# Attention scores as three rounded products of split q and k, with the unit's steps rearranged

## The chip, the cores and the metric

The program runs on one core of a Trainium2 chip. The metric is the device time in microseconds of one execution. Kernels are compared by the median of several runs. The profile comes from one further execution, whose own time is given beside its span.

## The reference, cut to what matters

Attention over 4 batches, 8 heads, 576 positions and 64 columns a head, with a bias that a small network computes from positions; then two feed-forward layers over 2304 tokens of width 512 (2048 and 1536 inner columns). All inputs and the output are float32.

```
scores = q @ k.T / sqrt(64)                                  # B, H, S, S
x      = log1p(|i - j|) / log1p(max(i, 1))
scores = scores + (relu(x @ w1 + b1) @ w2) per head          # the bias
attn   = softmax(scores);  o = attn @ v                      # B, H, S, 64
x      = o as (2304, 512)
h = x @ w_in;  x = (h * cos(h)) @ w_out                      # first layer
xn = rms_norm(x) * rms_g
out = (silu(xn @ w_gate) * (xn @ w_val)) @ w_out             # second layer
```

## The kernel before

The order of all instructions is written out by hand; each engine executes its own in that order, and semaphores on tiles hold an instruction until what it reads has been written and what it overwrites has been read.

There are three stages. The bias stage (the loop over `T`, 36 turns) makes features of 128 partitions by 576 columns, three of four on VectorE (L413) and one on ScalarE (L415), multiplies them on TensorE (L443), scales the result on ScalarE (L449) and writes it to memory; `load_bias` reads it back by heads. The features run two turns ahead. Three steps of the first attention unit are put into this loop, at T = 28, 31 and 35 (`STEP_AT`).

The attention stage runs over 16 units. A unit `u` is a pair of heads of one batch; its 9 row tiles of 576 queries (2 heads by 4.5 tiles of 128) are worked off in five steps `p`. In steps 0 to 3, `qk` (L217) computes the scores of a query tile of both heads: the two heads lie on partitions 0 to 63 and 64 to 127, and their matmuls run side by side on two halves of the rows of the array (row tiling, `tile_position=(64 * hh, 0)`). Step 4 takes the last half tiles of both heads in one matmul of full height (L222). All of this is float32, which is two instructions a matmul in the profile. `softmax` then adds the bias and takes the row maximum on VectorE (L231), which empties the PSUM tile of the scores (two such buffers), and takes the exponential and the row sum on ScalarE (L235). `tr` transposes the tile on TensorE against `ident` (L247, L251; L257, L260 for step 4) through three PSUM buffers, and copies it to `eT` on ScalarE and VectorE (L248, L252, L258). `av` multiplies by v (L278) with the two heads on two halves of the array's columns (column tiling), in two halves of a unit of 256 and 320 queries, each over five chunks of keys. `recip` takes the reciprocals of the sums, and has GpSimd spread them (`rw`, L290); `norm` transposes `rw` (L298), and `norm_out` multiplies (L313), rounds to float32r on ScalarE (`xh`, L315) and takes the remainder on GpSimd (`xl`, L316).

In `step(u, p)` the transposes are those of the step before (`tr(u, p - 1)`, in step 0 `tr(u - 1, 4)`), and `av` runs in all five steps: chunks 3 and 4 of the last unit's first half in step 0, its second half in steps 1 and 2, the first half of this unit's in steps 3 and 4. `load_k` and `load_q` put q and k of the next unit into double buffers in step 1.

The feed-forward stage (`run_item`, 140 items) multiplies by `mm3` (L508): both factors are split into a rounded float32r part and its remainder, and three of the four products are added up in PSUM. The weights come as 64-bit numbers in 68 pieces: `w_abs` on ScalarE (L105), `w_conv` on VectorE in two calls of two instructions each (L116 and L117, L120 and L121), `w_split` on ScalarE and GpSimd (L137, L138) into a ring of 1 + 9 buffers (`WA`, `WB`). From unit 4 on, two calls of `w_conv` and one of `w_tick` stand in each attention unit.

Of the kernel before, what the change touches and what calls it, by code (L numbers as in the profile page):

```python
# [7 lines left out]
F32 = mybir.dt.float32  # L8
F32R = mybir.dt.float32r
# [14 lines left out]
SPAN = 2 * S - 4  # L24
BLKS = [(0, 512), (512, 512), (2048, 256), (1024, 512), (1536, 512)]
# [6 lines left out]
WB = 9  # L32
# [19 lines left out]
def attn_moe(tc, qd, kd, vd, smallp, lrow, ident_d, wf1, wf2, rmsg, out):  # L52
# [56 lines left out]
    def w_conv():  # L109

        i = wstate["conv"]
        r = raw_t[i]
        hi, lo = r[:, :, 1], r[:, :, 0]
        t = w32_t[i]
        if not wstate["half"]:
            nc.vector.tensor_scalar(t.bitcast(F32), t.bitcast(F32), LEAST, GREATEST, op0=ALU.max, op1=ALU.min)  # L116
            nc.vector.tensor_scalar(t, t, 3, 0x3FFFFFFF, op0=ALU.logical_shift_left, op1=ALU.bitwise_and)  # L117
            wstate["half"] = 1
            return
        nc.vector.scalar_tensor_tensor(t, hi, -0x40000000, t, op0=ALU.bitwise_and, op1=ALU.bitwise_or)  # L120
        nc.vector.scalar_tensor_tensor(t, lo, 29, t, op0=ALU.logical_shift_right, op1=ALU.bitwise_or)  # L121
        raw_t.pop(i)
        wstate["half"] = 0
        wstate["conv"] += 1

    def w_split(eng=nc.gpsimd):
        i = wstate["split"]
        j = i % (WA + WB)
        if j < WA:
            t = wa.tile([128, 2, 512], F32R, tag="w", name="wA", bufs=WA)  # L130
        else:
# [38 lines left out]
    def load_k(u):  # L170
        if u < 16:
            hp, b = divmod(u, 4)
            kt = prep.tile([128, 640], F32, tag="k", name="kt", bufs=2)
            nc.sync.dma_start(kt, kd[b, hp])
            kq[u] = [kt, None]

    def load_q(u):
        if u < 16:
            hp, b = divmod(u, 4)
            qt_ = prep.tile([128, 640], F32, tag="q", name="qt", bufs=2)  # L180
            nc.sync.dma_start(qt_, qd[b, hp])
            kq[u][1] = qt_
# [20 lines left out]
    prep, st_prep = pool("prep")  # L203

    st = {}

    def qk(u, p):


        kt, qt_ = kq[u]  # L210
        if p < 4:
            pss = [psB.tile([128, 2, 512], F32, tag="S", name="psS", bufs=2) for _ in range(2)]
            for x in range(2):
                for hh in range(2):
                    r = slice(64 * hh, 64 * hh + 64)
                    k0 = 64 - 64 * hh + 288 * x
                    nc.tensor.matmul(pss[hh][:, x, 0:288], qt_[r, 128 * p:128 * p + 128], kt[r, k0:k0 + 288],  # L217
                                     start=True, stop=True, tile_position=(64 * hh, 0))
            return pss
        ps = psB.tile([128, 2, 512], F32, tag="S", name="psS", bufs=2)  # L220
        for x in range(2):
            nc.tensor.matmul(ps[:, x, 0:288], qt_[:, 512:640], kt[:, 64 + 288 * x:352 + 288 * x], start=True, stop=True)  # L222
        return [ps]
# [14 lines left out]
    def tr(u, p):  # L238
        s_ = st[u]
        e = s_["e"].pop(p)  # L240
        if p < 4:
            eT, q0 = (s_["eT0"], 128 * p) if p < 2 else (s_["eT1"], 128 * (p - 2))
            for c, ev in ((0, nc.scalar.copy), (2, nc.vector.tensor_copy)):
                pt = psA.tile([128, 512], F32, tag="tr", name="pt", bufs=3)
                for i in range(4):
                    k0 = 128 * (c + i // 2) + (S + 64) * (i % 2)
                    nc.tensor.transpose(pt[:, 128 * i:128 * i + 128], e[:, k0:k0 + 128], ident)  # L247
                ev(eT[:, 2 * c:2 * c + 4, q0:q0 + 128], pt.rearrange("p (c q) -> p c q", c=4))  # L248

            pt = psA.tile([128, 512], F32, tag="tr", name="pt", bufs=3)  # L250
            nc.tensor.transpose(pt[:, 0:128], e[:, 512:640], ident)  # L251
            nc.vector.tensor_copy(eT[:, 8, q0:q0 + 128], pt[:, 0:128])  # L252
        else:
            eT = s_["eT1"]
            pt = psA.tile([128, 512], F32, tag="tr", name="pt", bufs=3)
            for c in range(4):
                nc.tensor.transpose(pt[:, 128 * c:128 * c + 128], e[:, 128 * c:128 * c + 128], ident)  # L257
            nc.scalar.copy(eT[:, 0:8, 256:320], pt.rearrange("p (c q) -> p c q", c=8))  # L258
            pt = psA.tile([128, 512], F32, tag="tr", name="pt", bufs=3)
            nc.tensor.transpose(pt[:, 0:128], e[:, 512:640], ident)  # L260
            nc.vector.tensor_copy(eT[0:64, 8, 256:320], pt[0:64, 0:64])
            nc.vector.tensor_copy(eT[64:128, 8, 256:320], pt[64:128, 64:128])
# [30 lines left out]
    def norm(u, half):  # L293
        s_ = st[u]
        rp = psA.tile([128, 512], F32, tag="tr", name="rp", bufs=3)
# [4 lines left out]
        nc.scalar.copy(rbc[:, 0:256], rp[:, 0:256])  # L300
        s_["rbc", half] = rbc
# [5 lines left out]
    def norm_out(u, half):  # L307
# [4 lines left out]
        xt = ap.tile([128, 320], F32, tag="xt", name="xt", bufs=2)  # L312
# [15 lines left out]
    def step(u, p):  # L328
# [29 lines left out]
        if p == 2:
            if u > 0:
                av(u - 1, 1, [3, 4])  # L360
            recip(u, 0)
        if p == 4:
            av(u, 0, [2])
        if p == 3:
            av(u, 0, [0, 1])
        if p == 1 and u > 0:
            load_k(u + 1)
            load_q(u + 1)
        if u >= 4 and p in (0, 3):
# [56 lines left out]
    load_k(0)  # L426
    load_q(0)
# [4 lines left out]
    for T in range(NTT):  # L432
# [258 lines left out]
    def run_item(n, between=None):  # L691
# [18 lines left out]
        w_tick(lambda i: i < WA + WB or lastuse[pieces[i - WA - WB]] <= n - SPL,  # L710
# [4 lines left out]
    def rest():  # L715
        norm(15, 1)
# [89 lines left out]
```

## Time and profile before

| | |
|---|---|
| median of 3 runs | 1192.57 us (1191.5 to 1192.88) |
| profiled execution, own time | 1192.12 us |
| its span | 1190.3 us |
| bias stage with the first unit | 0 to about 72 us |
| attention, units 1 to 15 | about 72 to 333 us |
| feed-forward | about 333 us to the end |
| TensorE busy | 1173.7 us (99%) |
| VectorE, ScalarE, GpSimd busy | 825.6, 542.1, 351.6 us |
| granted TensorE clock | 1.00 in every stretch |

How to read it: PE is TensorE's matmuls, PEld its weight loads, DVE VectorE, ACT ScalarE, POOL GpSimd, SP SyncE, which issues DMAs. Ends of matmuls are modelled and overlap the next one's start, so distances from start to start tell the pace. L217 is line 217 of the kernel before.

### The profile page before, as it was taken

Reading aid. Unit: us, or ns where it says so; the run is one execution under the profiler, and the core shown is the slowest. Engines: PE = TensorE matmul, PEld = TensorE weight load, DVE = VectorE, ACT = ScalarE, POOL = GpSimd, SP = SyncE. Lnnn points to the kernel's source line nnn. Section 1 sums busy time; section 2 is a strip of 40 time slices with the busy share of each in tenths; the row PEclk is TensorE's granted clock in tenths of the full one; section 3 lists DMA queues with packets and bytes.
Section 4 is the critical chain, followed back from the end, with each engine's and each line's share of the span. In section 5 each row is a group of like instructions: output and inputs, shape, how many; then the busy total and the mean of one; then the engine's idle time right before and its main releaser. Section 6 shows DMA issues by size and latency. Waiting matters only on the chain.

```text
span 1190.3 us, 17685 instructions
## 1 busy us (share of the span) xinstructions
PE 1173.7 (99%) x6628; PEld 907.4 (76%) x6628; DVE 825.6 (69%) x1588; ACT 542.1 (46%) x1060; POOL 351.6 (30%) x373
## 2 busy tenths in 40 slices
PE   7999999999999999999999999999999999999998
PEld 3466666666678888888888887888888888888887
DVE  8966677777778789879879987885565355533232
ACT  7966667767654444445435546332222222222111
POOL 0011112222232244234234445663331232123111
PEclk9999999999999999999999999999999999999999
DMA  6833425362212011201201110111112011200012
GB/s 194 267 120 108 135 66 160 103 191 65 69 37 70 19 36 36 71 19 37 70 18 43 46 36 18 50 58 36 36 36 74 16 46 43 71 1 1 36 46 78
DMA packets 30852, 79.23 MB, mean 67 GB/s; under 512 B 3888, under 2 KB 4144, under 8 KB 30768
## 3 DMA queue, kind: packets, MB, share of 16 engines
q1 hardware_dynamic: 30480, 77.52, 20.8%
q8 instruction: 52, 0.85, 0.3%
q10 hardware_dynamic: 288, 0.59, 0.1%
q14 instruction: 32, 0.26, 0.1%
HBM read 62.76 MB, written 15.34 MB: 66 GB/s over the span
## 4 chain that ended last, share of the span: by engine, by line
PE 85%; DVE 8%; ACT 3%; issue 2%; DMA 1%; POOL 0%; SPq 0%; DVEq 0%; ACTq 0%; POOLq 0%
PE y L508 25%; PE h L508 13%; PE hg L508 12%; PE hv L508 12%; PE o L278 7%; PE psS L217 6%; PE pt L247 5%; PE psS L222 1%; DVE ft L413 1%; PE psb L443 1%; ACT G L449 1%; DVE yacc L611 1%; PE pt L257 1%; PE rp L298 1%; PE pt L251 1%
## 5 line engine op out<-in xcount | busy, mean ns | idle before, releaser
L508 PE MATMUL y<-g,wB 128*128 128x512 f32 (+1 forms) x960 | 213.4, 370 | 1.7 <-DVE yacc L611 1.2
L508 PEld LDWEIGHTS y<-g,wB 128*128 128x128 f32 x960 | 167.6, 188 | 34.4 <-DVE yacc L611 2.8
L558 POOL TENSOR_TENSOR g<-t,g 128x512 fp32r<-128x512 f32 (+1 forms) x80 | 98.1, 1227 | 236.8 <-ACT g L557 236.8
L575 POOL TENSOR_TENSOR g<-t,g 128x512 fp32r<-128x512 f32 (+1 forms) x60 | 74.1, 1235 | 292.3 <-ACT g L574 292.3
L231 DVE CUSTOM_DVE_ANT_0 e<-psS,bias 128x576 f32<-128x576 f32 x144 | 103.8, 753 | 63.6 <-PE psS L217 47.7
L508 PE MATMUL h<-xh,wB 128*128 128x512 f32 (+1 forms) x480 | 145.4, 369 | 0.0
L508 PE MATMUL y<-wB,g 128*128 128x512 f32 x594 | 143.5, 390 | 0.0
L235 ACT ACTIVATE e<-e,sm 128x576 f32<-128x576 f32 x144 | 110.6, 769 | 53.1 <-DVE sm L231 53.1
L508 PE MATMUL hv<-xh,wB 128*128 128x512 f32 (+1 forms) x440 | 133.7, 369 | 0.0
L508 PE MATMUL hg<-xh,wB 128*128 128x512 f32 (+1 forms) x440 | 133.2, 368 | 0.4 <-DVE t L570 0.4
L570 DVE TENSOR_TENSOR t<-t,hg 128x512 f32<-128x512 f32 (+1 forms) x60 | 38.0, 633 | 137.4 <-ACT t L569 137.4
L508 PEld LDWEIGHTS y<-wB,g 128*128 128x128 f32 x594 | 110.8, 188 | 22.5
L569 ACT ACTIVATE t<-hg 128x512 f32<-128x512 f32 (+1 forms) x60 | 33.3, 554 | 168.0 <-PE hg L508 161.8
L574 ACT CAST g<-t 128x512 fp32r<-128x512 f32 (+1 forms) x60 | 34.7, 578 | 164.5 <-DVE t L573 164.5
L508 PEld LDWEIGHTS h<-xh,wB 128*128 128x128 f32 x480 | 87.8, 188 | 16.0 <-issue 0.5
L552 ACT ACTIVATE r<-r 128x512 f32<-128x512 f32 (+1 forms) x80 | 47.2, 590 | 108.0 <-DVE r L549 107.7
L278 PE MATMUL o<-eT,v 128*64 128x256 f32 (+1 forms) x640 | 94.3, 416 | 0.0
L508 PEld LDWEIGHTS hg<-xh,wB 128*128 128x128 f32 x440 | 80.5, 188 | 15.0 <-DVE t L570 0.9
L138 POOL TENSOR_TENSOR wB<-w,wB 128x512 fp32r<-128x512 f32 x61 | 85.2, 1403 | 21.4 <-ACT wB L137 21.4
L508 PEld LDWEIGHTS hv<-xh,wB 128*128 128x128 f32 x440 | 80.6, 188 | 13.7
L557 ACT CAST g<-t 128x512 fp32r<-128x512 f32 (+1 forms) x80 | 46.2, 578 | 96.3 <-DVE t L556 87.9
L508 PE MATMUL h<-xl,wB 128*128 128x512 f32 (+1 forms) x240 | 88.4, 368 | 0.0
(116 smaller groups left out, 2130.8 us busy)
## 6 DMA issues: line engine op xcount, KB each, us to landing
raw<-in_wf_dram SPq DMA_DIRECT2D x68, 512.0 KB, 3.5
bdram<-G SPq DMA_DIRECT2D x36, 288.0 KB, 3.6
bias<-bdram SPq DMA_DIRECT2D x32, 288.0 KB, 3.3
kt<-in_kd_dram SPq DMA_DIRECT2D x16, 320.0 KB, 4.5
qt<-in_qd_dram SPq DMA_DIRECT2D x16, 320.0 KB, 5.1
v<-in_vd_dram SPq DMA_DIRECT2D x16, 320.0 KB, 3.9
out_dram<-yacc SPq DMA_DIRECT2D x16, 256.0 KB, 2.1
bias<-bdram SPq DMA_DIRECT2D x4, 144.0 KB, 3.3
```

Source lines behind the costliest of these rows:

```text
L138: eng.tensor_tensor(t[:, 1, :], r, t[:, 0, :].bitcast(F32), op=ALU.subtract)
L217: nc.tensor.matmul(pss[hh][:, x, 0:288], qt_[r, 128 * p:128 * p + 128], kt[r, k0:k0 + 288], start=True, stop=True, tile_position=(64 * hh, 0))
L231: nc.vector.tensor_tensor_reduce(out=e.rearrange("p (a b) -> p a b", a=2), in0=ps[:, :, 0:288], in1=bias_t[j].rearrange("p (a b) -> p a b" ...
L235: nc.scalar.activation(e, e, AF.Exp, bias=s_["m"][:, j:j + 1], scale=-1.0, accum_out=s_["sum"][:, j:j + 1])
L247: nc.tensor.transpose(pt[:, 128 * i:128 * i + 128], e[:, k0:k0 + 128], ident)
L278: nc.tensor.matmul(o[64 * hh:64 * hh + 64, 0:n], vt[:, c, 64 * hh:64 * hh + 64], eT[:, 2 * c + (hh if c < 4 else 0), :], start=(c == 0), s ...
L508: nc.tensor.matmul(ps, a, b_, start=(first and k == 0), stop=(last and k == tot - 1))
L552: nc.scalar.activation(r, r, AF.Abs)
L557: nc.scalar.copy(g[:, 0, :tn], t)
L558: nc.gpsimd.tensor_tensor(g[:, 1, :tn], t, g[:, 0, :tn].bitcast(F32), op=ALU.subtract)
L570: nc.vector.tensor_tensor(t, t, pg, op=ALU.mult)
L575: nc.gpsimd.tensor_tensor(g[:, 1, :tn], t, g[:, 0, :tn].bitcast(F32), op=ALU.subtract)
```

## The change

Scores become sums of three products of float32r parts: the rounded q by the rounded k, the rounded q by k's remainder, and q's remainder by the rounded k (`TERMS`), in units 1 to 15; unit 0 keeps one float32 product of the raw tiles. GpSimd makes the parts (`two_parts`): k of the next unit in step 2, into a double buffer; q by five slices of 128 columns into one buffer `qt_`, slices 0 to 3 in steps 3 and 4 of the unit before and slice 4 in step 0 of its own. The raw q and k of the next unit are loaded in step 0 into one buffer each; unit 1's are loaded and split in the bias stage, at T = 2.

In each step the transposes are now those of two steps before, the first group of them ahead of `softmax` and copied by ScalarE, the rest behind it. The last transposed tile of a step is copied by ScalarE instead of VectorE, and carries the transposes of `rw` where there are any. `av` of the last unit runs in steps 0 to 3. `w_conv` is cut into single instructions, one in each of steps 0, 1, 3 and 4. The ring of weights has 1 + 6 buffers, and 3 more from item 2 of the feed-forward stage on.

```diff
+TERMS = ((0, 0), (0, 1), (1, 0))
-WB = 9
+WB = 6
+WC = 3
+RING = WA + WB + WC
...
+    def load(u):
+        for k, src in enumerate((kd, qd)):
+            if u == 0:
...
+            else:
+                t = prep.tile([128, 640], F32, tag="raw" + "kq"[k], name="raw" + "kq"[k], bufs=1)
+            nc.sync.dma_start(t, src[u % 4, u // 4])
+            raw_kq[u, k] = t
...
+    def two_parts(t, raw):
+        nc.gpsimd.tensor_copy(t[:, 0, :], raw)
+        nc.gpsimd.tensor_tensor(t[:, 1, :], raw, t[:, 0, :].bitcast(F32), op=ALU.subtract)
+
+    def split_k(u):
+        t = prep.tile([128, 2, 640], F32R, tag="k", name="kt", bufs=2)
+        two_parts(t, raw_kq[u, 0])
+        kq[u] = [t, qt_]
+
+    def split_q(u, p):
+        c = slice(128 * p, 128 * p + 128)
+        two_parts(qt_[:, :, c], raw_kq[u, 1][:, c])
...
+    qt_ = prep.tile([128, 2, 640], F32R, name="qt")
...
+        kt, qt = kq[u]
+        terms = TERMS
+        if u == 0:
+            terms, kt, qt = ((0, 0),), kt.unsqueeze(1), qt.unsqueeze(1)
+        pss = [psB.tile([128, 2, 512], F32, tag="S", name="psS", bufs=2) for _ in range(2 if p < 4 else 1)]
+        for x in range(2):
+            for n, (a, b_) in enumerate(terms):
+                for hh, ps in enumerate(pss):
+                    r = slice(64 * hh, 64 * hh + 64) if p < 4 else slice(0, 128)
                     k0 = 64 - 64 * hh + 288 * x
+                    nc.tensor.matmul(ps[:, x, 0:288], qt[r, a, 128 * p:128 * p + 128], kt[r, b_, k0:k0 + 288],
+                                     start=(n == 0), stop=(n == len(terms) - 1), tile_position=(64 * hh, 0))
...
+        if first:
+            for i in range(4):
+                k0 = 128 * (i // 2) + (S + 64) * (i % 2) if p < 4 else 128 * i
+                nc.tensor.transpose(pt[:, 128 * i:128 * i + 128], e[:, k0:k0 + 128], ident)
+            nc.scalar.copy(eT[:, 0:512 // n, q0:q0 + n], pt.rearrange("p (c q) -> p c q", q=n))
+            return
...
+        nc.tensor.transpose(pt[:, 0:128], e[:, 512:640], ident)
+        if spread is not None:
+            norm(*spread, pt[:, 128:384])
+        if p < 4:
+            nc.scalar.copy(eT[:, 8, q0:q0 + n], pt[:, 0:128])
...
-        if u > 0 and p in (1, 3):
-            norm_out(u - 1, p // 2)
+        if u > 0 and p in (2, 4):
+            norm_out(u - 1, p // 4)
         pss = qk(u, p)
...
+        back = (u, p - 2) if p > 1 else (u - 1, p + 3)
+        if back[0] >= 0:
+            tr(*back, True)
         for j, ps in enumerate(pss, 2 * p):
             softmax(u, j, ps)
...
+        if back[0] >= 0:
+            tr(*back, False, (u, 0) if p == 4 else (u - 1, 1) if p == 2 and u > 0 else None)
+        if p == 2:
+            recip(u, 0)
+        if p == 0 and u > 0:
             recip(u - 1, 1)
...
+        if p < 4 and u > 0:
+            av(u - 1, p // 2, ([0, 1, 2], [3, 4])[p % 2])
+        if p == 0 and u > 1:
+            split_q(u, 4)
+        if 0 < u < 15:
+            if p == 0:
+                load(u + 1)
+            if p == 2:
+                split_k(u + 1)
+            if p > 2:
+                split_q(u + 1, 2 * p - 6)
+                split_q(u + 1, 2 * p - 5)
+        if u >= 4 and p != 2:
+            if wstate["conv"] < wstate["absd"]:
+                w_conv(1)
+            if p == 4:
                 w_tick(lambda i: i < WA + WB)
...
-        if T == 20:
-            load_k(1)
-        if T == 22:
-            load_q(1)
+        if T == 2:
+            load(1)
+            split_k(1)
+            for p in range(5):
+                split_q(1, p)
...
-    tr(15, 4)
+    tr(15, 3, True)
+    tr(15, 3, False)
     recip(15, 1)
-    av(15, 0, [3, 4])
+    av(15, 0, [0, 1, 2, 3, 4])
+    tr(15, 4, True)
+    tr(15, 4, False, (15, 1))
     run_item(0, rest)
```

## Rows read from the trace of the kernel before

**Rows 1.** The page: TensorE's busy time (us, share, instructions), the chain by engine.

```profile
PE 1173.7 (99%) x6628; PEld 907.4 (76%) x6628; DVE 825.6 (69%) x1588; ACT 542.1 (46%) x1060; POOL 351.6 (30%) x373
PE 85%; DVE 8%; ACT 3%; issue 2%; DMA 1%; POOL 0%; SPq 0%; DVEq 0%; ACTq 0%; POOLq 0%
```

**Rows 2.** Windows: stretch, length, busy us of PE, PEld, DVE, ACT, POOL; clock, DMA.

```profile
20.00:40.00 20.00, 20.00 (x233) 7.87 (x230) 20.00 (x48) 18.24 (x26) 0.00 (x0) 1.00 0.87 265
...
200.00:220.00 20.00, 20.00 (x148) 12.84 (x146) 15.49 (x43) 13.98 (x36) 3.92 (x6) 1.00 0.24 77
```

**Rows 3.** Timeline of TensorE, one attention unit: start us, us, what.

```profile
199.42 1.24 PE L217 MATMUL psS<-kt,qt 64*128 64x288 f32 x8
...
203.17 1.24 PE L217 MATMUL psS<-kt,qt 64*128 64x288 f32 x8
204.34 1.09 PE L247 MATMUL pt<-ident,e 128*128 128x128 f32 x8
...
206.49 1.24 PE L222 MATMUL psS<-kt,qt 128*128 128x288 f32 x4
207.56 0.38 PE L298 MATMUL rp<-ident,rw 128*128 128x128 f32 x2
...
208.82 0.33 PE L251 MATMUL pt<-ident,e 128*128 128x128 f32 x1
209.08 0.65 PE L278 MATMUL o<-eT,v 128*64 128x256 f32 x4
209.66 1.24 PE L217 MATMUL psS<-kt,qt 64*128 64x288 f32 x8
...
215.03 1.79 PE L278 MATMUL o<-eT,v 128*64 128x320 f32 x12
216.75 0.51 PE L217 MATMUL psS<-kt,qt 64*128 64x288 f32 x2
```

**Rows 4.** Chain of waits in the feed-forward stage: groups of 512, then 256 columns.

```profile
372.53 2.72 PE y L508 x12
375.25 1.43 PE h L508 x12
```

**Rows 5.** Groups of instructions by shape, 75 to 330 us: busy us, mean ns.

```profile
L316 POOL TENSOR_TENSOR xl<-xt,xh 128x320 fp32r<-128x320 f32 x15 | 13.0, 868 | 8.0 <-ACT xh L315 8.0
L290 POOL COPY rw<-sm 128x256 f32<-128x256 f32 x30 | 12.1, 404 | 131.4 <-DVE sm L288 127.4 <-PE psS L217 4.0
L316 POOL TENSOR_TENSOR xl<-xt,xh 128x256 fp32r<-128x256 f32 x15 | 11.0, 731 | 14.4 <-ACT xh L315 14.4
...
L237 POOL COPY e<-e 128x64 f32<-128x64 f32 x14 | 3.3, 236 | 28.4 <-ACT e L235 28.4
...
L252 DVE COPY eT<-pt 128x128 f32<-128x128 f32 x59 | 16.5, 280 | 0.0
...
L300 ACT COPY rbc<-rp 128x256 f32<-128x256 f32 x30 | 11.0, 367 | 21.0 <-PE rp L298 20.9
```

**Rows 6.** Timeline of VectorE and GpSimd in the feed-forward stage, two places.

```profile
336.53 0.43 DVE L548 TENSOR_SCALAR t<-t 128x512 f32<-128x512 f32 x1
...
343.26 1.30 POOL L558 TENSOR_TENSOR g<-t,g 128x512 fp32r<-128x512 f32 x1 [5.71 <-ACT g L557]
343.56 1.29 DVE L548 TENSOR_SCALAR t<-t 128x512 f32<-128x512 f32 x1
...
720.14 2.24 DVE L665 SCALAR_TENSOR_TENSOR yaccs<-yaccs,gcol,rb 128x256 f32<-128x256 f32 x2
...
720.62 1.48 POOL L138 TENSOR_TENSOR wB<-w,wB 128x512 fp32r<-128x512 f32 x1
```

**Rows 7.** Groups of VectorE in the bias stage; then its timeline there.

```profile
L413 DVE TENSOR_SCALAR ft<-L,nbp 128x576 f32<-128x576 f32 x117 | 50.6, 514 | 0.0
...
56.35 0.67 DVE L248 COPY eT<-pt 128x512 f32<-128x512 f32 x1
...
57.15 2.64 DVE L413 TENSOR_SCALAR ft<-L,nbp 128x576 f32<-128x576 f32 x6
...
71.43 0.76 DVE L231 CUSTOM_DVE_ANT_0 e<-psS,bias 128x576 f32<-128x576 f32 x1 [2.58 <-DMA bias<-bdram]
```

**Rows 8.** The page's DMA issues: count, KB each, us to landing.

```profile
qt<-in_qd_dram SPq DMA_DIRECT2D x16, 320.0 KB, 5.1
```

More of the change, by code (lines that the diff above doesn't have):

```diff
@@ L107, in w_abs, with w_conv @@
         wstate["abs"] += 1
[L109 to L124, printed above, removed]
+    def w_conv(quarters=2):
+        for _ in range(quarters):
+            i = wstate["conv"]
+            r = raw_t[i]
+            hi, lo = r[:, :, 1], r[:, :, 0]
+            t = w32_t[i]
+            if wstate["half"] == 0:
+                nc.vector.tensor_scalar(t.bitcast(F32), t.bitcast(F32), LEAST, GREATEST, op0=ALU.max, op1=ALU.min)
+            elif wstate["half"] == 1:
+                nc.vector.tensor_scalar(t, t, 3, 0x3FFFFFFF, op0=ALU.logical_shift_left, op1=ALU.bitwise_and)
+            elif wstate["half"] == 2:
+                nc.vector.scalar_tensor_tensor(t, hi, -0x40000000, t, op0=ALU.bitwise_and, op1=ALU.bitwise_or)
+            else:
+                nc.vector.scalar_tensor_tensor(t, lo, 29, t, op0=ALU.logical_shift_right, op1=ALU.bitwise_or)
+                raw_t.pop(i)
+                wstate["conv"] += 1
+            wstate["half"] = (wstate["half"] + 1) % 4
     def w_split(eng=nc.gpsimd):
         i = wstate["split"]
-        j = i % (WA + WB)
+        j = i % (WA + WB + WC)
         if j < WA:
             t = wa.tile([128, 2, 512], F32R, tag="w", name="wA", bufs=WA)
+        elif j >= WA + WB:
+            t = wstate["wc"].tile([128, 2, 512], F32R, tag="w", name="wC", bufs=WC)
         else:
@@ L168, in attn_moe @@
     vts = {}
[L170 to L182, printed above, removed]
+    raw_kq = {}
+    def load(u):
+        for k, src in enumerate((kd, qd)):
+            if u == 0:
+                t = rawp.tile([128, 512, 2], I32, tag="raw", name="first", bufs=NRAW)
+                t = t.rearrange("p a b -> p (a b)")[:, 0:640].bitcast(F32)
+            else:
+                t = prep.tile([128, 640], F32, tag="raw" + "kq"[k], name="raw" + "kq"[k], bufs=1)
+            nc.sync.dma_start(t, src[u % 4, u // 4])
+            raw_kq[u, k] = t
+        if u == 0:
+            kq[0] = [raw_kq[0, 0], raw_kq[0, 1]]
+    def two_parts(t, raw):
[8 more added lines that the diff above has]
+        two_parts(qt_[:, :, c], raw_kq[u, 1][:, c])
     bias_t = {}
@@ L203, in attn_moe @@
     prep, st_prep = pool("prep")
+    qt_ = prep.tile([128, 2, 640], F32R, name="qt")
     st = {}
     def qk(u, p):
[L210 to L215, printed above, removed]
-                    k0 = 64 - 64 * hh + 288 * x
[L217 to L223, printed above, removed]
+        kt, qt = kq[u]
+        terms = TERMS
+        if u == 0:
+            terms, kt, qt = ((0, 0),), kt.unsqueeze(1), qt.unsqueeze(1)
[4 more added lines that the diff above has]
+                    r = slice(64 * hh, 64 * hh + 64) if p < 4 else slice(0, 128)
+                    k0 = 64 - 64 * hh + 288 * x
+                    nc.tensor.matmul(ps[:, x, 0:288], qt[r, a, 128 * p:128 * p + 128], kt[r, b_, k0:k0 + 288],
+                                     start=(n == 0), stop=(n == len(terms) - 1), tile_position=(64 * hh, 0))
+        return pss
     def softmax(u, j, ps):
@@ L237, in softmax, with tr @@
             nc.gpsimd.tensor_copy(e2[:, S:S + 64], e2[:, S - 64:S])
-    def tr(u, p):
+    def tr(u, p, first, spread=None):
         s_ = st[u]
-        e = s_["e"].pop(p)
-        if p < 4:
[L242 to L248, printed above, removed]
-            pt = psA.tile([128, 512], F32, tag="tr", name="pt", bufs=3)
-            nc.tensor.transpose(pt[:, 0:128], e[:, 512:640], ident)
-            nc.vector.tensor_copy(eT[:, 8, q0:q0 + 128], pt[:, 0:128])
-        else:
[L254 to L262, printed above, removed]
@@ new lines, in tr @@
+        if first and p in (0, 2):
+            s_["eT", p // 2] = ap.tile([128, 9, 256 + 32 * p], F32, tag=f"eT{p}", name=f"eT{p}", bufs=1)
+        e = s_["e"][p]
+        eT, q0 = s_["eT", min(p // 2, 1)], 128 * (p % 2 if p < 4 else 2)
+        n = 128 if p < 4 else 64
+        pt = psA.tile([128, 512], F32, tag="tr", name="pt", bufs=3)
+        if first:
[4 more added lines that the diff above has]
+            return
@@ L264, in av @@
+        if p < 4:
+            nc.scalar.copy(eT[:, 8, q0:q0 + n], pt[:, 0:128])
+        else:
+            for r in (slice(0, 64), slice(64, 128)):
+                nc.vector.tensor_copy(eT[r, 8, q0:q0 + n], pt[r, r])
+        del s_["e"][p]
     def av(u, half, cs):
@@ L425, in attn_moe @@
     nc.vector.tensor_copy(cv[:, 1:2], pc[:, 0:1])
-    load_k(0)
-    load_q(0)
+    load(0)
     nc.sync.dma_start(ident, ident_d)
@@ L709, in run_item @@
         m, c, bi, fi = items[min(n, NI - 1)]
-        w_tick(lambda i: i < WA + WB or lastuse[pieces[i - WA - WB]] <= n - SPL,
+        w_tick(lambda i: i < WA + WB or n > 1 and (i < RING or lastuse[pieces[i - RING]] <= n - SPL),
                nsplit=2 if n < 6 or m == 2 else 1)
```

47 lines of the change are left out of this document (11 added, 36 removed).

## The prediction

> **What bounds the kernel now.** I read the page first: the busy lines and the chain that ended last [rows 1]. TensorE is busy 99% of the span and the chain runs through it for 85%; but matmul ends are modelled, so a busy TensorE says little. I then took the span in stretches [rows 2]: in 20 to 40 us (the bias stage) VectorE is busy for all of the 20 us, in 200 to 220 us (attention) VectorE has 15.5, ScalarE 14.0 and GpSimd 3.9 of 20. The next view is TensorE alone over one attention unit [rows 3]. The reader is to look at starts only: a unit runs from 199.42 to 216.75, 17.33 us, and each group starts where the one before it has streamed out. A scores group of full height, L222, goes to its follower in 1.07 us (206.49 to 207.56). The row-tiled scores group, L217, takes 1.17 (203.17 to 204.34): the 0.10 more is what it costs to go from a tiled array to an untiled one, since L222's follower is untiled too. Fourteen such switches stand in a unit. The 12 passes of L278 with 320 columns from 215.03 to 216.75, less one switch, are six pairs of 0.27. Nothing here waits on another engine for long. So attention is bound by TensorE's streaming and switching; the bias stage ahead of it by VectorE, and at its end by the DMA of the last bias [rows 7].
>
> **Scores in three rounded products.** Before, a step's scores are four slots of float32: 1.07 less a first weight load of 0.10, so 0.242 a slot (0.27 at 320 columns, less 32 columns at two cycles, agrees). After, they are six slots of float32r. The feed-forward rows give that price [rows 4]: 12 matmuls of 512 columns in 2.72 us, 12 of 256 in 1.43, so 0.2267 and 0.1192 each, 0.42 ns a column; 288 columns cost 0.1327, six slots 0.80. A step saves 0.97 - 0.80 = 0.17. Five steps in units 1 to 15 (unit 0 keeps float32): 75 x 0.17 = **-12.8 us**. The ends: without the constant 13 ns a slot, -6.0 more; if the two weight loads of a row-tiled pair go one after the other (0.20 a pair), +28.9 (rival 4). I take the middle: L217 already runs pairs in the time of one L222 group.
>
> **v in four of five steps.** Step 4 of a unit loses its group of L278 (209.08 to 209.66, four passes). The passes move to another step, the switch into them and their first load don't: 0.58 - 2 x 0.2155 = 0.15 a unit, **-2.3 us** over 15. (0.2155 is 0.27 less 64 columns.)
>
> **Transposes two steps behind.** Their number stays: per unit 41 and 4 for the reciprocals, 0.109 each. No exp is waited for any more; rows show no such wait of weight in before, so I count nothing for it. But the pipeline is deeper. In unit 0 the kernel before does tr(0,3) and three chunks of v while VectorE waits 2.58 us for the last bias to land [rows 7]: free. After, this work follows at the end, after unit 15, where TensorE is the bound: 9 x 0.109 + 6 x 0.2155 + 0.15 = **+2.4 us**. For the same reason, tr(0,0) leaves the bias stage: its two copies on VectorE, from 56.35 to 57.15, go out of the stretch where VectorE is saturated, -0.8 to -0.9 (I take **-0.9**).
>
> **Copies shifted to ScalarE.** Four copies of 128 columns a unit leave VectorE (0.28 each [rows 5]) and reach ScalarE (at most the 0.37 of its copy of 256 columns). VectorE's 13.4 us of a 17.33 unit (15.49/20) becomes 12.3, ScalarE's 12.1 becomes at most 13.6, against a unit of 16.3: hidden behind TensorE. The cover is thin where step 4 has no v: TensorE there has 0.90 + 11 x 0.109 + 0.10 = 2.2 us before the next unit's scores need the buffer that VectorE empties, and that chain takes about 2.0. What is late next is the third transposed tile of step 0, released by ScalarE's last copy of step 4: 0 to 0.2 us a unit. A wait of this kind was there before: 0.26 us between L251 and L278 at 208.82, and L251 itself 0.2 late. So I count it as before, 0 (ends -1.8 and +1.8).
>
> **The splitting of q and k on GpSimd.** Twelve new instructions a unit. Two-input ones: 0.868 at 320 columns and 0.731 at 256 give 2.1 ns a column [rows 5], so 1.55 at 640 and 0.46 at 128. Copies: 0.404 at 256, 0.236 at 64: 0.73 and 0.29; no row shows one that rounds, at worst it costs what two inputs cost. Sum 6.0 us a unit (worst 7.7), on an engine that had 3.9 of 20. On time: after the reciprocal of step 2 GpSimd does rw 0.40, k 2.28, the first slice of q 0.75, so 3.4; the next unit's first scores come after step 3 (3.37) and step 4 (2.2), some 5.6 later. The two raw loads, issued in step 0, land in about 5.1 us [rows 8], 6 us before k's split in step 2. The load of raw q waits for q's last slice on GpSimd (about 1.1 us after the reciprocal); behind it on SyncE's queue stand the bias loads of the last unit of a head pair and the weight loads, both a unit early. Cost 0; if that cover is gone, rival 3.
>
> **What this does to VectorE.** GpSimd and VectorE exclude each other on some operations [rows 6]: the L548 operation takes 0.43 alone and 1.29 when a GpSimd instruction of 1.30 has begun 0.3 earlier. At 720 us back-to-back VectorE instructions and GpSimd ones take turns: two L665 of only 256 columns took 2.24 around a GpSimd instruction of 1.48 that began between them. So a GpSimd instruction of 1.30 costs VectorE 1.29 - 0.43 = 0.86, some 0.65 of its length. The first place is the bias stage: unit 1 is split at T = 2, among 117 features of 0.514 without a gap on VectorE. Cost 0.65 x 6.0 = **+3.9 us**; ends 0 (GpSimd gets no turn until the features pause) and 6.0. The second is the weight conversion, now four single instructions a unit in 10 units: each can wait up to 0.86, 3.4 us a unit, which keeps VectorE at 15.7 of 16.3. I take 0.15 a unit on the path, **+1.5**; ends 0 and one whole wait a unit, 8.6. The Trainium skill (SBUF — State Buffer, section "SBUF: two separate sides") says that the pair of ports is held for the whole instruction and the loser fully blocks. By that rule the bias stage would lose the full 6.0; the 0.86 of 1.30 says less. I keep it as rival 2.
>
> **The ring of weights.** Seven instead of ten pieces are ready when the feed-forward stage begins; three are split in items 2 and 3, 2.8 us of GpSimd beside its 1.3 per item, in items of 5.4 us (two groups of 2.72). Hidden; 0, ends -0.3 and +1.
>
> **Sum.** -12.8 - 2.3 + 2.4 - 0.9 + 3.9 + 1.5 = -8.2 on the profiled 1192.12 us (span 1190.3): 1183.9. The median of the runs is 0.45 above the profiled time: **1184.4**.
>
> **Rivals.** (1) Quicker: no constant per slot (-6.0), GpSimd gets its turns only in pauses (-3.9, -1.5): 1173. For it: a float32 pass shows hardly a constant; against: every float32r row has one, and at 720 us GpSimd got its turn. (2) The locks hold in full: +2.1 in the bias stage, +7.1 in attention: 1193.6. For it the rule and the 1.29; against, that most GpSimd instructions are short slices. (3) Slower: GpSimd's chain rw, k, q slice 0 ends last at a unit's first scores. It decides once it takes 2.2 us more than the 3.4 counted; if the copies cost what two inputs do (+1.0) and each of the five instructions waits 0.5 for VectorE, it takes 6.9, 1.3 late in 15 units, +19.5: 1203.9. The same would follow if a read of one slice of q waited for the writing of another. Against: these slots are 60% free. (4) Paired weight loads in series: 1213. Against: pairs in before hide theirs.
>
> **Chances.** Forecast 0.62 (own range 1178 to 1190), rival 1 0.10, rival 2 0.12, rival 3 0.10, rival 4 0.06. The range 1174 to 1198 leaves out part of 1, most of 3 and 4. A change under 0.2% (2.4 us) can't be told from none; faster 0.73 (forecast, rival 1, a little of 2), within 0.10, slower 0.17.
>
> **What would show it.** Right: the scores group's start to its follower's start at 1.0 (tiled) and 0.9 (full), a unit of 16.2 to 16.4 us, features in the bias stage longer than 0.514 beside GpSimd, attention beginning about 3.0 later, the tail after unit 15 longer by 2.4. Wrong: a unit over 17 us with TensorE's scores released by GpSimd (rival 3), scores slots of 0.21 (rival 4), features untouched.

## The result and the profile after

The changed kernel takes 1179.05 us (median of 4 runs, 1178.45 to 1180.24), the kernel before 1192.03 beside it: ratio 0.9892, interval 0.9875 to 0.9909, so 13.0 us faster. The profiled execution of after took 1179.05 us, its span is 1177.0 (before: 1190.3).

The page says little: TensorE's busy share and the chain's shares stay within two points of where they were [rows 1]. GpSimd has grown by 122.6 us, ScalarE by 10.3.

```profile
PE 1157.9 (98%) x6898; PEld 917.0 (78%) x6898; DVE 819.8 (70%) x1524; ACT 552.4 (47%) x1124; POOL 474.2 (40%) x553
PE 84%; DVE 10%; ACT 3%; issue 2%; DMA 1%; SPq 0%; POOL 0%; DVEq 0%; ACTq 0%
```

The timeline of TensorE over a unit of after, against [rows 3]. L240 is the scores, L268, L274 and L277 are transposes, L301 multiplies by v.

```profile
201.24 1.06 PE L240 MATMUL psS<-kt,qt 128*128 128x288 f32 x6
202.13 0.60 PE L268 MATMUL pt<-ident,e 128*128 128x128 f32 x4
...
203.43 1.06 PE L240 MATMUL psS<-kt,qt 64*128 64x288 f32 x12
204.42 0.66 PE L268 MATMUL pt<-ident,e 128*128 128x128 f32 x4
...
205.55 1.51 PE L301 MATMUL o<-eT,v 128*64 128x256 f32 x12
207.00 1.06 PE L240 MATMUL psS<-kt,qt 64*128 64x288 f32 x12
...
217.27 0.93 PE L240 MATMUL psS<-kt,qt 128*128 128x288 f32 x5
```

The unit (201.24 to 217.27) is 16.03 us; it was 17.33. A tiled scores group goes to its follower in 0.99 (1.17 before), the full-height one in 0.89 (1.07). No idle time is marked between two groups.

To see where the 13.3 us of span went, I follow the scores' starts and the first feed-forward matmul, in TensorE's timelines of both kernels. Before (L217 tiled scores, L508 feed-forward):

```profile
61.81 1.24 PE L217 MATMUL psS<-kt,qt 64*128 64x288 f32 x8
...
75.12 1.24 PE L217 MATMUL psS<-kt,qt 64*128 64x288 f32 x8
...
316.58 1.26 PE L217 MATMUL psS<-kt,qt 64*128 64x288 f32 x8
...
332.75 0.50 PE L508 MATMUL h<-xh,wA 128*128 128x512 f32 x1
```

After:

```profile
57.62 5.80 PE L455 MATMUL psb<-ft,small 128*32 128x512 f32 x64 [2.08 <-DVE sm L250]
63.36 1.24 PE L240 MATMUL psS<-first 64*128 64x288 f32 x8
...
73.61 1.05 PE L240 MATMUL psS<-kt,qt 64*128 64x288 f32 x11 [2.33 <-DVE sm L250]
76.06 2.81 PE L301 MATMUL o<-eT,v 128*64 128x256 f32 x12
78.81 1.06 PE L240 MATMUL psS<-kt,qt 64*128 64x288 f32 x12
...
299.57 1.06 PE L240 MATMUL psS<-kt,qt 64*128 64x288 f32 x12
303.14 1.06 PE L240 MATMUL psS<-kt,qt 64*128 64x288 f32 x12
...
320.14 0.47 PE L521 MATMUL h<-xh,wA 128*128 128x512 f32 x1
```

| stretch | before | after | difference |
|---|---|---|---|
| start of step 2 of unit 0 | 61.81 | 63.36 | +1.55 |
| from there to step 1 of unit 1 | 13.31 | 15.45 | +2.14 |
| 14 units, step 1 to step 1 | 241.46 | 224.33 | -17.13 |
| step 1 of unit 15 to the feed-forward | 16.17 | 17.00 | +0.83 |
| the rest of the span | 857.55 | 856.86 | -0.69 |

The second row holds something new. Step 0 of unit 1 takes 5.20 (73.61 to 78.81), that of unit 15 only 3.57: 1.63 lost. The 12 passes of L301 at 76.06 take 2.75 to the next start, where they take 1.45 in the unit above. The windows of after say why (length; busy us of PE, PEld, DVE, ACT, POOL; clock; DMA share, GB/s):

```profile
20.00:40.00 20.00, 20.00 (x233) 7.80 (x233) 20.00 (x48) 18.07 (x26) 20.00 (x1) 1.00 0.88 265
...
57.60:60.00 2.40, 2.38 (x24) 0.90 (x28) 2.40 (x7) 2.40 (x6) 0.00 (x0) 0.64 0.15 57
...
71.00:73.60 2.60, 0.29 (x1) 0.07 (x1) 0.81 (x3) 0.00 (x0) 0.00 (x0) 1.00 0.72 221
...
75.00:77.00 2.00, 2.00 (x14) 1.29 (x14) 1.97 (x7) 1.71 (x4) 0.00 (x0) 0.58 0.18 70
...
200.00:220.00 20.00, 20.00 (x177) 14.65 (x178) 16.99 (x43) 16.47 (x43) 12.73 (x24) 1.00 0.25 77
```

TensorE stands idle for 2.08 us before 57.62 and for 2.33 before 73.61, and some time after each the clock falls towards its lower level (0.5 is 1.2 GHz, 1.00 is 2.4): 0.64 from 57.6 us on, 0.58 from 75 us on, where it was still 1.00 from 73.6 to 75. In before it is 1.00 in all these windows.

### The profile page after: what moved, and what is told of

It reads as the page before. It is cut to its first block, busy times and chain, and to the rows that moved or that the text cites. A ratio compares the mean times of both kernels' runs of the same rounds, so it can differ in the third digit from the quotient of the medians.

```text
span 1177.0 us, 18382 instructions
## 1 busy us (share of the span) xinstructions
PE 1157.9 (98%) x6898; PEld 917.0 (78%) x6898; DVE 819.8 (70%) x1524; ACT 552.4 (47%) x1124; POOL 474.2 (40%) x553
## 4 chain that ended last, share of the span: by engine, by line
PE 84%; DVE 10%; ACT 3%; issue 2%; DMA 1%; SPq 0%; POOL 0%; DVEq 0%; ACTq 0%
PE y L521 25%; PE h L521 14%; PE hg L521 12%; PE hv L521 12%; PE o L301 7%; PE psS L240 6%; PE pt L268 4%; PE pt L274 2%; DVE ft L426 2%; PE psb L455 2%; DVE yacc L624 1%; DVE t L561 1%; PE pt L277 1%; DVE r L562 1%; DVE w L123 1%
## 5 line engine op out<-in xcount | busy, mean ns | idle before, releaser
L250 DVE CUSTOM_DVE_ANT_0 e<-psS,bias 128x576 f32<-128x576 f32 x144 | 104.1, 755 | 58.1 <-PE psS L240 53.4
L521 PE MATMUL y<-g,wB 128*128 128x512 f32 (+1 forms) x600 | 133.4, 370 | 1.2 <-DVE yacc L624 1.2
L521 PEld LDWEIGHTS y<-g,wB 128*128 128x128 f32 x600 | 105.0, 188 | 21.5 <-DVE yacc L624 2.4
L521 PE MATMUL h<-xh,wB 128*128 128x512 f32 (+1 forms) x360 | 109.1, 369 | 0.0
L521 PE MATMUL hv<-xh,wB 128*128 128x512 f32 (+1 forms) x320 | 97.1, 369 | 0.0
L301 PE MATMUL o<-eT,v 128*64 128x256 f32 (+1 forms) x640 | 91.8, 418 | 0.0
L521 PE MATMUL y<-wB,g 128*128 128x512 f32 x378 | 91.4, 389 | 0.0
L240 PEld LDWEIGHTS psS<-kt,qt 64*128 64x128 f32 (+1 forms) x810 | 62.0, 185 | 31.7 <-issue 21.0
L240 PE MATMUL psS<-kt,qt 64*128 64x288 f32 (+1 forms) x810 | 79.8, 309 | 2.3 <-DVE sm L250 2.3
L521 PEld LDWEIGHTS y<-wB,g 128*128 128x128 f32 x378 | 70.5, 188 | 14.3
L521 PE MATMUL y<-g,wC 128*128 128x512 f32 (+1 forms) x360 | 79.9, 370 | 0.1
L586 DVE TENSOR_TENSOR t<-t,hv 128x512 f32<-128x512 f32 (+1 forms) x60 | 38.0, 633 | 58.5 <-PE hv L521 58.4
```

Source lines behind the costliest of these rows:

```text
L240: nc.tensor.matmul(ps[:, x, 0:288], qt[r, a, 128 * p:128 * p + 128], kt[r, b_, k0:k0 + 288], start=(n == 0), stop=(n == len(terms) - 1), t ...
L250: nc.vector.tensor_tensor_reduce(out=e.rearrange("p (a b) -> p a b", a=2), in0=ps[:, :, 0:288], in1=bias_t[j].rearrange("p (a b) -> p a b" ...
L521: nc.tensor.matmul(ps, a, b_, start=(first and k == 0), stop=(last and k == tot - 1))
L586: nc.vector.tensor_tensor(t, t, pv, op=ALU.mult)
```

## The experiments

All are edits of the changed kernel. A unit's length is the distance between the starts of the same scores group in two units.

**One float32 product instead of three.**

```diff
-TERMS = ((0, 0), (0, 1), (1, 0))
+TERMS = ((0, 0),)
...
-qt[r, a, 128 * p:128 * p + 128], kt[r, b_, k0:k0 + 288],
+qt[r, a, 128 * p:128 * p + 128].bitcast(F32), kt[r, b_, k0:k0 + 288].bitcast(F32),
```

> The changed kernel, but with one float32 product of the rounded parts of q and k instead of three rounded products (both remainders are left out of the scores); the splitting on GpSimd and the order stay. Theory (the three products pay by TensorE's slots alone): a step's scores go from six slots of 0.131 to four of 0.242, +0.18 a step, 75 steps, so 13 us slower than the changed kernel's 1179.05: 1192, about the kernel before; a unit goes from 16.02 to 16.9. Rival (the gain comes mostly from the new order, because nothing waits any more): under 5 us slower, 1184 or less.

Measured 1192.7 us, ratio to before 1.0002 (0.9993 to 1.0011); units of 16.93 instead of 16.02. All else of the change stays in, and the whole gain is gone: the scores are worth 13.65 us (0.91 a unit, 0.18 a step), and everything else together nothing, as gains and losses that cancel.

**The old order of transposes and v, with the split scores.** The step is before's, with transposes one step behind and v in five steps:

```diff
-        back = (u, p - 2) if p > 1 else (u - 1, p + 3)
-        if p < 4 and u > 0:
-            av(u - 1, p // 2, ([0, 1, 2], [3, 4])[p % 2])
+        if p > 0:
+            tr(u, p - 1)
+        elif u > 0:
+            tr(u - 1, 4)
+            av(u - 1, 0, [3, 4])
...
+        if p == 4:
+            av(u, 0, [2])
+        if p == 3:
+            av(u, 0, [0, 1])
```

> The changed kernel with the order of the steps of the kernel before: transposes one step behind, v in all five steps, reciprocals' transposes in a tile of their own, the copies of 128 columns on VectorE; the splitting and the three products stay. Theory: a unit takes 16.02 + 0.15 (switch and first load of the fifth v group) and up to 0.22 where a weight piece is split, so 16.2 to 16.4, +2.5 to +5.5 over 15 units; the shorter pipeline gives back 1.5 at the end and about 1.5 of slow clock at unit 1: 1179 to 1182. Rival (the new order is what hides GpSimd and the locks): units over 16.8, the time above 1188.

Measured 1177.16, ratio 0.9874 (0.9861 to 0.9888), below the 1179 to 1182 expected: the new order does not pay. TensorE's timeline, a unit from full-height scores to full-height scores, then the end of attention:

```profile
200.71 1.06 PE L240 MATMUL psS<-kt,qt 128*128 128x288 f32 x6
...
216.91 0.80 PE L240 MATMUL psS<-kt,qt 128*128 128x288 f32 x4
...
300.69 1.06 PE L240 MATMUL psS<-kt,qt 64*128 64x288 f32 x12
...
318.82 0.50 PE L531 MATMUL h<-xh,wA 128*128 128x512 f32 x1
```

A unit is 16.20, so the new order saves 0.18 in each of 14 (-2.5); which of its parts does it is not separated. But from unit 15's start to the feed-forward it is 18.13 here and 20.57 in after: the deeper pipeline costs +2.44. And here the idle before unit 1 is 1.18 us, with the clock at 1.00 in the windows on both sides:

```profile
71.00:73.60 2.60, 1.71 (x13) 0.94 (x11) 0.54 (x1) 0.22 (x1) 0.00 (x0) 1.00 0.72 212
73.60:75.00 1.40, 1.12 (x12) 0.95 (x13) 1.06 (x5) 1.08 (x3) 0.15 (x1) 1.00 0.97 371
```

**Unit 1 split behind the bias stage.** The raw loads stay at T = 2; `split_k(1)` and the five `split_q(1, p)` go behind the loop over T.

> The changed kernel, with the splitting of unit 1's q and k put behind step 2 of unit 0 in GpSimd's order (the loads stay at T = 2). Theory (GpSimd's eleven instructions between 50 and 57 us hold up ten features of VectorE by 1.7, and TensorE, left idle, loses its clock there): features back at 0.44 apart, no clock under 1.00 between 57 and 63, step 2 of unit 0 starts at 61.0 to 61.8 instead of 63.36; 1.5 to 2.3 us less, 1177. Rival (the end of the bias stage is set by the DMA chain of the biases): under 0.5 less.

Measured 1177.36, ratio 0.9875 (0.9862 to 0.9889). VectorE and GpSimd in after's timeline at the end of the bias stage show what the early place does, L191 and L192 being the two parts:

```profile
19.26 30.84 POOL L191 CAST kt<-rawk 128x640 fp32r<-128x640 f32 x1 [14.33 <-DMA rawk<-in_kd_dram]
49.44 0.75 DVE L250 CUSTOM_DVE_ANT_0 e<-psS,bias 128x576 f32<-128x576 f32 x1
50.18 1.56 POOL L192 TENSOR_TENSOR kt<-rawk,kt 128x640 fp32r<-128x640 f32 x1
50.80 6.10 DVE L426 TENSOR_SCALAR ft<-L,nbp 128x576 f32<-128x576 f32 x10
```

GpSimd's copy of k, 0.72 in the 14 later units, lasts from 19.26 to 50.10. In 20 to 40 VectorE still ends 48 instructions, as before [rows 2]: GpSimd lost, the features did not. The copy ends in the first pause of the features: VectorE does 88 of them in a row, and then, at 49.44, the softmax of unit 0's step 0; 0.66 us later the copy is done (0.66 or 0.67 in e1_f32_scores, e4_warm, e5_no_split and e6_copy_dve too). After this pause GpSimd gets its turns among the features as well, and ten features take 6.10. With the split moved away, the same features in e3_split_late:

```profile
50.17 4.38 DVE L426 TENSOR_SCALAR ft<-L,nbp 128x576 f32<-128x576 f32 x10
...
60.81 1.24 PE L240 MATMUL psS<-first 64*128 64x288 f32 x8
```

1.72 less, and step 2 of unit 0 starts at 60.81 instead of 63.36. The median falls by 1.69; the rest of the 2.55 between the two starts is mostly spread between profiles, since the softmax of step 0 already began 0.62 earlier here (48.82). The slow clock at 57.6 us is gone too (1.00 there); the one in unit 1 stays (idle of 2.99 us).

**TensorE kept busy before unit 1.** 24 transposes of `ident` into a spare tile, ahead of the scores of step 0 of unit 1.

> The changed kernel with 24 transposes of the identity, read by nobody, ahead of unit 1's first scores, where TensorE has nothing to do for 2.3 us. Theory (the idle stretch halves TensorE's clock at 75 to 79 us): the clock stays at 1.00 there, v's 12 passes at 76.06 take 1.3 instead of 2.81, and the time falls by 1.2 to 1.7, to 1177.6. Rival (those passes wait for v or for copies): the clock and the 2.81 stay, no gain; or the dummies delay the scores, up to 0.3 more.

Measured 1177.07, ratio 0.9873 (0.9859 to 0.9886). TensorE's timeline:

```profile
70.22 2.84 PE L360 MATMUL warm<-ident 128*128 128x128 f32 x24
72.99 1.08 PE L241 MATMUL psS<-kt,qt 64*128 64x288 f32 x12
75.13 1.52 PE L302 MATMUL o<-eT,v 128*64 128x256 f32 x12
76.58 1.06 PE L241 MATMUL psS<-kt,qt 64*128 64x288 f32 x12
```

The clock stays 1.00 in 71 to 77 us, step 0 takes 3.59 instead of 5.20, and the median falls by 2.0 us. The loss in this step was the slow clock, and work without a use in the idle stretch is enough to keep the clock up here.

**No splits on GpSimd from unit 2 on.** `load`, `split_k` and `split_q` of step give way to `kq[u + 1] = kq[1]`.

> The changed kernel without the loads and the splitting of q and k for units 2 to 15, which all use unit 1's (their scores are those of unit 1). Theory (in attention, GpSimd's 6 us a unit and the turns it takes with VectorE are wholly hidden): units stay at 16.02 and the time within 0.5 of 1179.05. Rival (VectorE's or GpSimd's turns hold TensorE up in small pieces): units under 15.9, 1.5 us or more less.

Measured 1177.72, ratio 0.9873 (0.9856 to 0.9889). Its window beside after's 12.73 of GpSimd:

```profile
200.00:220.00 20.00, 20.00 (x177) 14.66 (x178) 16.24 (x43) 16.46 (x44) 4.91 (x7) 1.00 0.14 44
```

GpSimd falls by 7.8 us and VectorE by 0.75, but units stay 16.02: in attention the splitting is hidden, turns and all. The median is 1.33 below after, more than the 0.5 expected. The units do not hold it: the profiled execution, with its units of 16.02, took 1178.67, and the four runs lie between 1176.12 and 1179.08. Where the shorter ones gained is not shown.

**The last copy back on VectorE** (`nc.vector.tensor_copy` for L281).

> The changed kernel with the four copies of 128 columns a unit back on VectorE. Theory (the shift to ScalarE is free either way, TensorE being the bound): units of 16.0 to 16.3, 1179 to 1183. Rival (VectorE then ends last in step 4, where no v covers it): 0.28 a step or more on the path, units over 16.5, above 1186.

Measured 1179.23, ratio 0.9888 (0.9873 to 0.9902), units 16.02. The shift to ScalarE is worth nothing. Its profile shows something else, of the clock (TensorE's timeline, then a window):

```profile
56.96 4.38 PE L455 MATMUL psb<-ft,small 128*32 128x512 f32 x56 [2.07 <-DVE sm L250]
57.60:60.00 2.40, 2.40 (x45) 1.31 (x40) 2.40 (x6) 2.40 (x7) 0.00 (x0) 1.00 0.00 0
```

TensorE was idle for 2.07 us, as in e1_f32_scores, e4_warm and e5_no_split, which show 0.50 to 0.59 in this window; here the clock is 1.00, and stays so until 63 us. So the length of an idle stretch does not decide by itself, and what else does is left open.

**The split late, and real transposes to fill the idle.** `tr(0, 3)` and 18 dummies go ahead of step 0 of unit 1.

> The changed kernel with three edits at the first units: unit 1's splitting behind step 2 of unit 0 as in the split_late run, unit 0's step-3 transposes moved ahead of unit 1's first scores, where TensorE has nothing to do, and 18 dummy transposes behind them. Theory: the 1.7 of split_late, the 2.0 of warm and 0.85 for the nine transposes that leave TensorE's bound stretch (the next step is then held by VectorE's chain of 2.7) add up: 1174.5. Rival (they overlap, since all three shorten the same idle stretch): 1176 or more.

Measured 1180.19, ratio 0.9897 (0.9882 to 0.9912): 1.1 slower than after, where 4.5 less was expected. Its timeline:

```profile
71.37 0.76 DVE L251 CUSTOM_DVE_ANT_0 e<-psS,bias 128x576 f32<-128x576 f32 x1 [3.52 <-DMA bias<-bdram]
72.80 0.66 PE L275 MATMUL pt<-ident,e 128*128 128x128 f32 x4 [3.30 <-DVE eT L276]
74.06 3.51 PE L362 MATMUL warm<-ident 128*128 128x128 f32 x18
```

The second group of transposes needs a PSUM tile that VectorE empties, and that copy is queued behind the softmax that waits for the last bias. The dummies stand behind this group, so TensorE is idle for 3.30 and slow after (0.50 in 73.6 to 75). A filler must wait for nothing.

**Old order with the late split.**

> The order of the kernel before with the three products and the splitting, as in the old_order run, and unit 1's splitting behind step 2 of unit 0. Theory (the 1.7 of split_late is won in the bias stage and does not depend on the order): 1175.5, units of 16.20. Rival (in this order TensorE kept its clock, and the gain of split_late was the clock): 1176.8 or more.

Measured 1175.42, ratio 0.9860 (0.9846 to 0.9875): e2_old_order less 1.7.

**New order, late split and 28 dummies.**

> The changed kernel with both edits of split_late and warm, with 28 dummy transposes, which stand ahead of everything that can wait. Theory (the first removes GpSimd's turns from the bias stage, 1.7; the second the slow clock after TensorE's idle stretch ahead of unit 1's scores, which split_late still had, 1.5): 1175.6 to 1176. Rival (the dummies are too many for the stretch, or both edits win the same time): 1177 or more.

Measured 1175.97, ratio 0.9865 (0.9852 to 0.9879), with the clock at 1.00 from 50 to 84 us: 3.1 less than after, most of what the two edits gain alone (1.7 and 2.0).

**Mixed order.** Late split; unit 0 runs in the old order, which fills the idle with its own work and takes it out of unit 1's first two steps; from then on the new one.

```diff
+        if u == 0:
+            back = (0, p - 1) if p > 0 else (-1, 0)
+        elif (u, p) == (1, 0):
+            back = (-1, 0)
...
-        if p < 4 and u > 0:
+        if u == 0 and p > 2:
+            av(0, 0, [0, 1] if p == 3 else [2])
+        elif (u, p) == (1, 0):
+            av(0, 0, [3, 4])
+        elif p < 4 and u > 0 and (u, p) != (1, 1):
```

> The changed kernel with unit 1's splitting late, and unit 0 in the order of the kernel before (transposes one step behind, v of its first half in its steps 3 and 4 and in step 0 of unit 1), from step 2 of unit 1 on in the changed order. Theory (both orders are worth what they were found to be: units of 16.02, the idle of unit 0 filled with work that the tail need not do; steps 0 and 1 of unit 1 then last 2.7 each, held by VectorE's chain): about 1.3 less than old_late's 1175.42: 1174.1. Rival (what the deeper pipeline needs at the end, it needs whatever stands at the start; the lag is paid once in either case): 1175.4 to 1176.

Measured 1173.95 (1173.82 to 1174.27), ratio 0.9849 (0.9835 to 0.9862), the best of all. TensorE waits 0.98 before unit 1, and the clock is 1.00 from end to end:

```profile
71.94 1.05 PE L240 MATMUL psS<-kt,qt 64*128 64x288 f32 x11 [0.98 <-DVE sm L250]
...
315.61 0.47 PE L529 MATMUL h<-xh,wA 128*128 128x512 f32 x1
```

The tail is not shorter: from the full-height scores of unit 15 to the feed-forward it is 6.73 here (from 308.88) and in after (313.41 to 320.14). The gain lies at unit 1.

**The weight conversion in pairs again**, in the old and in the mixed order:

```diff
-        if u >= 4 and p != 2:
+        if u >= 4 and p in (0, 3):
             if wstate["conv"] < wstate["absd"]:
-                w_conv(1)
-            if p == 4:
+                w_conv()
+            if p == 3:
```

> The kernel before's order of a unit, with the split scores, the late split of unit 1 and the weight conversion put back to two pairs of VectorE instructions a unit (steps 0 and 3) instead of four single ones. It asks where the 0.22 us a unit went by which the eight later units of the kernel before (17.33 from score to score) were longer than the six earlier ones (17.11). Theory (the pair on VectorE delays the copies of the transposes, and the transposes wait for their PSUM tile): the later eight units go from 16.20 to about 16.42, the first six stay at 16.20, and the time goes from 1175.42 (the same with single instructions) to 1177.2. Rival (the 0.22 came from something else, such as the longer scores or the double loads of q and k): 16.20 in all units, 1175.4.

> The mixed order (unit 0 in the old order, the later units in the new one) with the weight conversion put back to two pairs of VectorE instructions a unit. Theory (in the new order the copies of the transposes have a whole step more, so a pair of conversions delays nothing that is waited for): units stay at 16.02 and the time at 1174.0. Rival (a pair costs 0.22 in either order): later units 16.24, 1175.7.

Measured 1179.31, ratio 0.9882 (0.9866 to 0.9899), against 1175.42 with single ones; and 1176.79, ratio 0.9865 (0.9850 to 0.9879), against 1173.95. In the old order seven units go from 16.20 to 16.6 (16.42 expected); in the mixed order nine go from 16.02 to 16.2, where I had expected nothing. In e11_old_pairs 1.07 of the loss lies ahead of unit 1, which the edit does not reach; that part is left open.

The edit moves two things: with the pairs, `w_tick` goes back from step 4 to step 3, where the kernel before has it. For the old order the traces tell them apart. ScalarE and TensorE's weight loads in before, at the wait of 208.82 [rows 3]:

```profile
207.30 0.62 ACT L137 CAST wB<-w 128x512 fp32r<-128x512 f32 x1
207.82 0.69 ACT L105 ACTIVATE w<-raw 128x512 f32<-128x512 f32 x1
208.42 0.34 ACT L300 COPY rbc<-rp 128x256 f32<-128x256 f32 x1
208.82 0.14 PEld L251 LDWEIGHTS pt<-ident,e 128*128 128x128 f32 x1 [0.24 <-ACT rbc L300]
```

The last transposes of step 4 go into the PSUM tile that held the transposed reciprocals, and ScalarE empties that tile late, behind the two weight instructions of `w_tick` (L137 rounds a piece, L105 is `w_abs` of another). In e11_old_pairs (TensorE's timeline) the same copy, L319, releases them:

```profile
202.37 0.33 PE L270 MATMUL pt<-ident,e 128*128 128x128 f32 x1 [0.17 <-ACT rbc L319]
```

VectorE's pair stands in step 4 of ten units there, but the seven longer units are those in which ScalarE has both weight instructions ahead of that copy. The units from 167.25 and from 299.63 have the pair and only one of the two, and take 16.20 and 16.21. Before, the eight longer units likewise are those with L137 ahead of the copy; the one from 171.99 has the pair without L137, and takes 17.11. In e8_old_late, with `w_tick` in step 4, the copy runs at 199.96 and the weight instructions from 201.76 on. So in the old order the place of `w_tick` cost the time, and the pairs nothing.

The mixed order is another case. There the scores at 198.97 take 1.19 to their follower instead of 0.99 (VectorE, then TensorE):

```profile
196.48 0.70 DVE L123 SCALAR_TENSOR_TENSOR w<-raw,w 128x512 int32<-128x512 int32 x1
197.21 0.83 DVE L125 SCALAR_TENSOR_TENSOR w<-raw,w 128x512 int32<-128x512 int32 x1
...
198.37 0.74 DVE L250 CUSTOM_DVE_ANT_0 e<-psS,bias 128x576 f32<-128x576 f32 x1
...
198.97 1.26 PE L240 MATMUL psS<-kt,qt 64*128 64x288 f32 x12
200.16 0.66 PE L268 MATMUL pt<-ident,e 128*128 128x128 f32 x4
```

Here I read it as the scores' second PSUM buffer, which L250 empties late, after the pair: it ends at 199.04, where in e10_hybrid it ends 0.41 before its scores start. All nine longer units have the pair, and two of them only one weight instruction of `w_tick`; a run with the pairs alone is missing. So single instructions avoid a loss that the new order would have had. What before lost, it lost by `w_tick`.

## Why the prediction was right, and where it was not

Forecast 1184.4, measured 1179.05. The mechanism and the sign were right; these are its terms:

| term | predicted | measured | from |
|---|---|---|---|
| scores, 75 steps | -12.8 | -13.65 | one float32 product |
| v in four of five steps | -2.3 | -2.5 | 16.20 against 16.02, 14 units (the whole new order) |
| deeper pipeline, tail | +2.4 | +2.44 | 20.57 against 18.13 |
| GpSimd's turns in the bias stage | +3.9 | +1.7 | medians: e3_split_late against after, e8_old_late against e2_old_order |
| tr(0,0) out of the bias stage | -0.9 | -0.6 | step 2 of unit 0: mean 61.06 of 3 profiles (new order, late split) against 61.64 of 5 (old order, no early split) |
| weight conversion in single instructions | +1.5 | 0 | e5_no_split: units stay 16.02 |
| the wait at 208.82 | 0 | -1.8 | 17.33 against 17.11, 8 units |
| slow clock in unit 1 | not seen | +1.63 | 5.20 against 3.57 |
| feed-forward | 0 | -0.69 | spans |

The measured terms add up to -13.5; the medians differ by 13.0, the spans by 13.3. The forecast's sum was -8.2; the other part of its distance is the 0.45 by which I put the median above the profiled time. Part of the nearness is luck: the weight work came out 3.3 lower than forecast and the turns 2.2, and the slow clock, which the forecast did not count, took 1.63 of that back.

**Scores.** The price came from the feed-forward's float32r rows [rows 4], and six slots cost 0.18 less than four passes, not 0.17. Tiled pairs stream at this price too, so rival 4 (weight loads in series) is out.

**v and the pipeline.** Both sized right as far as the runs separate them, and together they cancel: -2.5 and +2.44. What the new order leaves is the slow clock, and that makes it a loss: e2_old_order is 1.9 us faster than the changed kernel. The prediction saw that the work of unit 0 had stood free under the wait for the last bias [rows 7], and charged it to the tail. It did not ask what TensorE does in the 2 us that this work had filled.

**The bias stage.** The prediction had both ends (no turn until the features pause, or the full 6.0); the traces show the first for 30 us and turns for the last six. There ten features lost 1.72 to GpSimd instructions that take 5.3 us when alone (1.56, and ten of 0.292 and 0.460 in turn), so 0.32 of their length and not 0.65. The 0.65 was read too low in itself: in [rows 6] the GpSimd instruction had run for 0.30 of its 1.30 when VectorE's began, so 0.86 was lost of the 1.00 that was left. The two starts 63.36 and 60.81 would give 2.55 and not 1.7, but kernels alike up to there differ as well: 62.49 to 63.36 in five with the early split, 60.81 to 61.43 in three with the late one. The term for tr(0,0) is good to about half a microsecond for the same reason. The Trainium skill (SBUF — State Buffer, section "SBUF: two separate sides") lets whichever engine starts first hold the shared ports while the other blocks; the 30.84 us of one GpSimd copy, which ended in VectorE's first pause, fit a blocked loser, but no run tells why the two took turns afterwards, when features again followed one another.

**The weight work.** This is the step that failed, in sign. I looked at what four single instructions could lose to GpSimd (+1.5). e5_no_split shows that GpSimd's turns cost the units nothing, so rivals 2 and 3 are out in attention: GpSimd has 12.7 of 20 us, and with 4.9 the units are as long. And I had seen the 0.26 us at 208.82, a wait for ScalarE, and carried it along as unchanged ("ends -1.8 and +1.8"). But the change moves `w_tick`, with its two ScalarE instructions, from step 3 to step 4, behind the copy that TensorE waits for, and the wait is gone: the lower end was the measured value. With the old order this move is enough: all units of e2_old_order take 16.20.

**What would show it.** Scores at 1.0 and 0.9: 0.99 and 0.89. Units 16.2 to 16.4: 16.02, because the wait at 208.82 went and the single instructions cost nothing. Features longer than 0.514: only the last ones. Attention 3.0 later: 1.55 at step 2 of unit 0, and 3.69 at step 1 of unit 1, of which 1.63 is the slow clock. Tail longer by 2.4: 2.44 against the old order.

## What to carry to other kernels

Before a step's work is moved out of a wait, ask what the engine then does in that wait: an idle TensorE may come back at half the clock, and the price stands in the next step, not in the wait. Helper work on a busy in-order engine belongs behind the copies that others wait for: two weight instructions ahead of one small copy cost 0.2 us a unit before, and a pair ahead of a softmax 0.2 in the mixed order. And test the parts of a change alone: here one of them made the gain, one added to it unnoticed, and the rearrangement took a little back. An edit that puts two parts back at once blames either; units that happen to have only one of them can tell.

## What the runs showed of the hardware

- One GpSimd copy, 0.72 us in later units, lasted 30.84 us beside back-to-back VectorE instructions, while these kept their pace, and ended in their first pause; after that the two engines alternated.
- After TensorE had been idle for 2.08 and 2.33 us (after) and 2.99 us (e3_split_late) the granted clock fell to between 0.50 and 0.72; after 0.98, 1.18 and 1.64 us before unit 1 (e10_hybrid, e2_old_order, e11_old_pairs) it stayed 1.00. Idle stretches of 2.07 us went both ways: 0.50 to 0.59 in three kernels, 1.00 in e6_copy_dve. Transposes of a constant tile (24 in 2.77 us) kept it at 1.00.
- Six slots of 288 columns in float32r cost 0.18 us less than four float32 passes, row-tiled or not (0.99 against 1.17, 0.89 against 1.07).
